# Loading the ninth token group as seven tokens a partition, one batch on each half of the partitions

## The chip, the core and the metric

The kernel runs on one core of a Trainium2 chip. The metric is the device time of one execution in microseconds (us), lower is better; three executions of the kernel before are given below. The core has five engines with instruction queues of their own: PE (TensorE, matrix products and transposes), DVE (VectorE), ACT (ScalarE), POOL (GpSimd) and SP (SyncE, which here only issues transfers), and 16 DMA engines that move data between the chip's memory and the on-chip memory of 128 partitions.

## The reference

A gated recurrence over 5056 tokens in 4 batches of 256 channels is followed by a mixture of 8 experts with 4 slots each ("soft" slots: every token takes part in every slot).

```python
sig = 1.0 / (1.0 + np.exp(-f_logit))
f = lower_bound + (1.0 - lower_bound) * sig
h = f[:, t] * h + (1.0 - f[:, t]) * x[:, t]      # for t in range(5056); y[:, t] = h

x = y.reshape(4 * 5056, 256)
logits = x @ phi                                  # 32 slots
d = softmax of logits over the tokens (axis 0)
slot_input = d.T @ x                              # 32 x 256
slot_out[e] = np.maximum(slot_input[e] @ w1[e], 0) @ w2[e]
c = softmax of logits over the slots (axis 1)
out = c @ slot_out                                # 20224 x 256, f32
```

## The kernel before

**Groups and units.** The 5056 tokens of a batch are cut into ten groups (`n_grp`) of 512 tokens; the last group begins at 5056 - 512, so the ninth (`odd`, index 8) keeps only 448 tokens. A *unit* is one group of one batch, numbered 0 to 39; units 32 to 35 are the ninth group in its four batches, and units are loaded and partly computed in pairs (32 with 33, 34 with 35). Units 8 to 31 are "long": a pair of them is two successive groups of one batch, loaded as eight tokens a partition.

**One unit, step by step.** `load` (L204) brings `f_logit` into `f_t` and `x` into `x_t` with transfers that SP issues; each tile holds a pair and each has three buffers, so SP waits until the pair three before has been used. `gate` (L227) computes the sigmoid of a pair into `s_t` on ACT. `enter` (L237) multiplies it with `x_t` into `u_t` on POOL. PE then transposes `s_t` (`s_to_channels`) and `u_t` (`u_to_channels`) from tokens on partitions to channels on partitions, two bf16 channels as one f32 value. `decay` (L286) turns the transposed sigmoid into the decay factors `a` on ACT. `scan` (L306) runs the recurrence along the tokens on DVE and writes `h`. `to_tokens` (L320) transposes `h` back on PE, `keep_tokens` (L336) copies it out of PSUM into `ht`, alternately on ACT and DVE. Once per one or two groups, `logits` multiplies `h` with `phi`, `exps` takes the exponential into `etall`, and `slots` adds up the slot inputs.

**The order of the work.** It is written out by hand, in the loop `for n in range(n_unit)` (L484): each pass issues the scan of unit n, the transposes of unit n + 1, `gate` up to four units ahead, `enter` three units ahead, and `load` six units ahead (`AHEAD`). Each engine runs its queue in that order. The weights of the experts are loaded by POOL's queue (`load_w`, L135) at the passes listed in `W_AT` (L155): one each at passes 9, 17, 25, 31 and 32, two at 33, three at 34 and six at 36; the last one comes in three pieces. They are cast from f32 to bf16 on the way.

**The ninth group.** A batch's 448 tokens are 3 x 128 + 64 (`R3` = 3, `L` = 64). Three tokens a partition of each batch of a pair go to `t[:, m, 0:3]`. The last 64 tokens of both batches share one column of 128 rows, `t[:, 0, 3]`, even rows for one batch and odd rows for the other (L216). The column is transposed once for each batch against an identity with its columns regrouped (`sides`, L252 to L256), which puts that batch's 64 tokens behind its 384.

**After the last scan.** The last groups' exponentials and slot inputs are finished, then come the experts: `hi` (first matrix, L628), transposed `ht_ps` (L643), copied into `hid` and `wide` (L646 to L660), and the second matrix for four experts at a time (L664, and L674 for the experts in `wide`). `row_sums` (L386) and filler matmuls (`spin`, L150) stand between the products. `slot_out` (L692) is the result.

**The output.** `out` is made in blocks of 16 tokens a partition (and one of 7): `whole` (L723) does one batch, `couple` (L738) two batches at a time, with copies out of PSUM on DVE and ACT. `ends` says after which token columns a part is stored; without it a couple is stored once, at its end. A couple's first part goes out as one transfer a batch (L768), a later part as one for both (L765). `rest` stores the 64 tokens that no block holds. At the start, ten small matmuls (L467 to L469) run on PE between the constants and the first unit.

Of the kernel before, what the change touches and what calls it, by code (L numbers as in the profile page):

```python
# [9 lines left out]
F32 = mybir.dt.float32  # L10
# [3 lines left out]
ACT = mybir.ActivationFunctionType  # L14
# [4 lines left out]
def kernel(  # L19
# [26 lines left out]
    def first(g):  # L46
        return g * G if g < n_grp - 1 else S - G
# [72 lines left out]
    etall = store.tile([P, S + PAD], BF16, name="etall")[:, :S]  # L120
    rrow = store.tile([P, n_grp * R, B], F32, name="rrow")
    left = store.tile([P, L, 2], BF16, name="left")
    nc.vector.memset(left, 0.0)
    csum = store.tile([P, n_grp], F32, name="csum")
    nc.vector.memset(csum, 0.0)
    w1_r = moe_w1.rearrange("e (p o) f -> e p o f", o=DC)
# [35 lines left out]
    with tc.tile_pool(name="sp2", bufs=3) as sp2, \  # L162
# [24 lines left out]
        def long(n):  # L187
            return 2 * B <= n < n_unit - 2 * B
# [15 lines left out]
        def load(n, k=2):  # L204
            for src, dst, tag in ((f_logit, fs, "f_t"), (x, xs, "x_t")):
                if n % 2 == 0:
                    dst[n // 2] = ld.tile([P, 2, R, D], F32, name=tag, tag=tag)
                t = dst[n // 2]
                if long(n):
                    g, b = place(n)  # L210
                    nc.sync.dma_start(
                        out=t.rearrange("p u r d -> p (u r) d"),
                        in_=src[b, ds(first(g), 2 * G)].rearrange("(p r) d -> p r d", r=2 * R))
                elif n // B == odd:
                    b, t0 = n % B, first(odd)
                    nc.sync.dma_start(  # L216
                        out=t[:, 0, R3],
                        in_=src[ds(b, 2), ds(t0 + P * R3, L)].rearrange("b t d -> t b d"))
                    for m in range(2):
                        nc.sync.dma_start(  # L220
                            out=t[:, m, ds(0, R3)],
                            in_=src[b + m, ds(t0, P * R3)].rearrange("(p r) d -> p r d", r=R3))
                else:
                    for m in range(n, n + k):
                        nc.sync.dma_start(out=t[:, ds(m % 2, 1)], in_=tokens(src, m, 1))
# [11 lines left out]
        def enter(n):  # L237
            uts[n] = sup.tile([P, R, D], BF16, name="u_t", tag="u_t")
            s_t, x_t = sts[n // 2][:, n % 2], xs[n // 2][:, n % 2]
            if n == 0:  # L240
                for r in range(0, R, 2):
                    nc.vector.tensor_tensor(uts[n][:, ds(r, 2)], s_t[:, ds(r, 2)],
                                            x_t[:, ds(r, 2)], ALU.mult)
            else:
                r = R3 if n // B == odd and n % 2 else R
                nc.gpsimd.tensor_tensor(uts[n][:, :r], s_t[:, :r], x_t[:, :r], ALU.mult)  # L246

        def to_channels(n, ps, t, rest):
            t = t.bitcast(F32)
            if n // B == odd:  # L250
                flat = ps.rearrange("c p r -> c (p r)")
                sides = ident_f.rearrange("p (t u) -> p u t", u=2)  # L252
                v = flat[:, ds(0, P * R3)].rearrange("c (p r) -> c p r", r=R3)
                k = P * R3 - n % 2 * L
                nc.tensor.matmul(flat[:, ds(k, P)], rest.bitcast(F32), sides,
                                 is_transpose=True, start=True, stop=True)  # L256
                for r in range(R3):
                    nc.tensor.transpose(v[:, :, r], t[:, r], ident_f)
                return
            for r in range(R):  # L260
                nc.tensor.transpose(ps[:, :, r], t[:, r], ident_f)  # L261

        def half_to_channels(n, ps, t):
            k = ds(n % 2 * (P // 2), P // 2)
            v = ps.rearrange("c p r -> c (p r)").rearrange("c (p r) -> c p r", r=2 * R)
            for r in range(2 * R):
                nc.tensor.transpose(v[:, :, r], t(r)[k].bitcast(F32), ident_f[k, k])  # L267

        def s_to_channels(n):
            if n % 2 == 0:  # L270
                pss[n // 2] = psp.tile([P, 2, P, R], F32, name="sp", tag="sp")
            to_channels(n, pss[n // 2][:, n % 2], sts[n // 2][:, n % 2],
                        sts[n // 2][:, 0, R3])

        def u_to_channels(n):
            ps = psu.tile([P, P, R], F32, name="up", tag="up")
            if long(n):
                half_to_channels(n, ps, lambda r: uts[n - n % 2 + r // R][:, r % R])
            else:
                to_channels(n, ps, uts[n], uts[n - n % 2][:, R3])  # L280
            psus[n] = ps.rearrange("c p r -> c (p r)").bitcast(BF16).rearrange(
                "c (t o) -> c t o", o=DC)

# [2 lines left out]
        def decay(n, k=2, os=range(DC)):  # L286
            T = used(n // B)
            sp = pss[n // 2].rearrange("c u p r -> c u (p r)").bitcast(BF16)
            if long(n):
                sp = sp.rearrange("c u (p r o) -> c p u r o", r=R, o=DC)  # L290
                for o in os:
                    decays[n // 2, o] = apool.tile([P, 2, G], F32, name="a", tag=f"a{o}")
                    a = decays[n // 2, o].rearrange("c u t -> c (u t)").rearrange(
                        "c (p u r) -> c p u r", u=2, r=R)
                    nc.scalar.activation(a, sp[:, :, :, :, o], ACT.Identity,  # L295
                                         scale=nomlb[:, ds(o, 1)], bias=1.0)
                return
            sp = sp.rearrange("c u (t o) -> c u t o", o=DC)
            for o in os:
                if n % 2 == 0:  # L300
                    decays[n // 2, o] = apool.tile([P, 2, G], F32, name="a", tag=f"a{o}")
                nc.scalar.activation(decays[n // 2, o][:, ds(n % 2, k), :T],  # L302
                                     sp[:, ds(n % 2, k), :T, o], ACT.Identity,
                                     scale=nomlb[:, ds(o, 1)], bias=1.0)
# [159 lines left out]
        for n in range(SINGLE):  # L464
            load(n, 1)
        lb_constants()
        for _ in range(10):  # L467
            nc.tensor.matmul(slot_bank[:, 1, ds(0, NS)], ident, ident[:, :NS],
                             start=True, stop=True, skip_group_check=True)  # L469
        gate(0, 1)  # L470
        enter(0)
        s_to_channels(0)
# [131 lines left out]
    with tc.tile_pool(name="ew", bufs=1) as ew, \  # L604
# [34 lines left out]
        for q in range(E // Q):  # L639
            ht_ps = psu.tile([P, FC, P], BF16, name="ht_ps", tag="up")  # L640
            hi_v = his[q].rearrange("p (c f) -> p f c", f=FC)
            for fc in range(FC):
                nc.tensor.transpose(ht_ps[:, fc], hi_v[:, fc], ident)  # L643
            if q == 0:
                nc.tensor.matmul(cs_ps, rep2, cs1, start=True, stop=True)
                src = ht_ps.rearrange("p f (j s) -> p f j s", s=NS)[:, :, :, ds(0, SPE)]  # L646
                src = bass.AP(tensor=src.tensor, offset=src.offset,
                              ap=[list(src.ap[0]), [P, FC], [NS + SPE, Q], [1, SPE]])
                dst = hid[:, :, :, ds(0, SPE)]
                dst = bass.AP(tensor=dst.tensor, offset=dst.offset,  # L650
                              ap=[list(dst.ap[0]), [Q * NS, FC], [NS + SPE, Q], [1, SPE]])
                nc.scalar.copy(dst, src)
                nc.vector.reciprocal(rcs, cs_ps)
                continue
            for j in range(Q):
                s0 = (Q + j) * SPE
                src = ht_ps[:, :, ds(j * NS + s0, SPE)]
                copy = nc.scalar.copy if j % 2 == 0 else nc.vector.tensor_copy
                copy(wide[:, :, j, :, ds(s0, SPE)],
                     src.unsqueeze(2).broadcast_to([P, FC, B, SPE]))  # L660
        so4_ps = pm.tile([P, D], F32, name="so4_ps", tag="pm")
        for e in range(Q):
            for fc in range(FC):
# [34 lines left out]
    with tc.tile_pool(name="osb", bufs=3) as osb:  # L698
# [39 lines left out]
        def couple(i, j, ends=()):  # L738
# [7 lines left out]
            for r in range(n_r):  # L746
# [11 lines left out]
                        scale[:, r].unsqueeze(2).broadcast_to([P, 2, D]), ALU.mult)  # L758
                if r + 1 in ends:
                    q = ds(done, r + 1 - done)  # L760
                    if done:
                        both = out[ds(2 * j * S, 2 * S)].rearrange(
                            "(u t) d -> u t d", u=2)[:, ds(t0, P * n_r)].rearrange(
                            "u (p r) d -> p u r d", r=n_r)
                        nc.sync.dma_start(out=both[:, :, q], in_=ob[:, :, q])  # L765
                    else:
                        for u in range(2):
                            nc.sync.dma_start(out=rows_of(i, 2 * j + u)[:, q],  # L768
                                              in_=ob[:, u, q])
                    done = r + 1  # L770
# [59 lines left out]
```

## Time and profile before

| | |
|---|---|
| three executions | 197.22, 197.34, 198.04 us (median 197.34) |
| the profiled execution | 197.27 us, of it span 195.5 us from first to last instruction |
| busy in the span | PE 152.8, DVE 147.2, ACT 137.3, POOL 103.3 us |
| mean granted TensorE clock | 0.859 of full speed |
| DMA | 70.75 MB written in 14145 packets; HBM read 58.23 MB, written 20.71 MB |

The page of the profile gives busy time by engine, the span in 40 slices, the DMA queues, the chain of waits that ended last, and the costliest groups of instructions. A group's line reads: source line, engine, operation, output and input tiles, shapes, count, then busy time in us and mean ns of one instruction, then the idle time of the engine before them and what ended it. A timeline's line reads: start in us, duration, engine, source line, operation and tiles, count, and in brackets the idle time before it. "w_t" and "w_sb" are the experts' weights; `SPq` is SP's queue.

### The profile page before, as it was taken

How to read it: one execution, taken by the hardware profiler on the slowest of the kernel's cores; microseconds unless marked ns; L12 is line 12 of the kernel's file. 1: busy time of each engine (PE TensorE's matmuls, PEld its weight loads, DVE VectorE, ACT ScalarE, POOL GpSimd, SP SyncE). 2: the span in 40 equal slices, each digit the busy share in tenths (PEclk: the TensorE clock that was granted, in tenths of full speed). 3: DMA queues.
4: the chain of work that ended last, by engine and by line, in shares of the span. 5: the costliest groups of instructions: out<-in, count | busy, mean ns of one | idle time of the engine just before them, and what ended most of it. 6: DMA issues, size and time to landing. Idle time of an engine off the chain costs nothing.

```text
span 195.5 us, 3260 instructions
## 1 busy us (share of the span) xinstructions
PE 152.8 (78%) x1205; PEld 105.0 (54%) x1205; DVE 147.2 (75%) x188; ACT 137.3 (70%) x188; POOL 103.3 (53%) x78
## 2 busy tenths in 40 slices
PE   1687589977998979899797887989999999990000
PEld 1465448765685767668586675557974433220000
DVE  2669858999889999999999999814279897771000
ACT  3688674899998998989987597544069987682000
POOL 2589578575999779774969969392030000000000
PEclk9999958999999999999999999999995555555555
DMA  6999999999999999999999999999939999999995
GB/s 206 421 417 424 429 424 429 429 422 393 341 424 431 416 322 427 427 408 347 366 423 413 260 213 214 215 215 213 164 148 420 427 454 419 436 432 429 429 429 221
DMA packets 14145, 70.75 MB, mean 362 GB/s; under 512 B 1569, under 2 KB 2594, under 8 KB 10162
## 3 DMA queue, kind: packets, MB, share of 16 engines
q1 hardware_dynamic: 11504, 62.13, 76.8%
q0 software_dynamic: 2624, 8.42, 21.6%
q8 instruction: 9, 0.15, 0.3%
q14 instruction: 6, 0.05, 0.1%
q10 hardware_dynamic: 2, 0.00, 0.0%
HBM read 58.23 MB, written 20.71 MB: 404 GB/s over the span
## 4 chain that ended last, share of the span: by engine, by line
PE 37%; DVE 26%; ACT 11%; DMA 8%; issue 5%; POOL 2%; SPq 0%; ACTq 0%; DVEq 0%; POOLq 0%
DVE h L313 20%; PE op L748 10%; DMA f_t<-in_f_logit_dram 8%; DVE ht L343 5%; PE hp L326 4%; ACT oc L753 4%; PE sp L261 3%; ACT s_t L235 3%; PE up L267 3%; PE lg L357 2%; POOL u_t L246 2%; PE op L711 2%; PE slot_ps L183 2%; PE so_ps L674 2%; PE slot_ps L408 1%
## 5 line engine op out<-in xcount | busy, mean ns | idle before, releaser
L246 POOL TENSOR_TENSOR u_t<-s_t,x_t 128x1024 bf16<-128x1024 bf16 (+1 forms) x39 | 82.5, 2132 | 23.6 <-ACT s_t L235 10.4
L313 DVE TENSOR_TENSOR_SCAN h<-a,h,up 128x512 bf16<-128x512 f32 (+1 forms) x72 | 87.0, 1252 | 3.5 <-PE up L267 1.8
L235 ACT ACTIVATE s_t<-f_t 128x2048 bf16<-128x2048 f32 (+2 forms) x23 | 38.3, 1668 | 4.0 <-DMA f_t<-in_f_logit_dram 3.7
L326 PE MATMUL hp<-ident_f,h 128*128 128x128 f32 (+1 forms) x160 | 29.4, 308 | 7.9 <-DVE ht L343 6.8
L326 PEld LDWEIGHTS hp<-ident_f,h 128*128 128x128 f32 (+1 forms) x160 | 23.6, 207 | 18.1 <-DVE ht L343 12.4
L748 PE MATMUL op<-slot_bd,etall 64*128 64x512 bf16 x62 | 26.4, 581 | 1.0 <-ACT oc L753 0.3
L295 ACT ACTIVATE a<-sp,lbs 128x1024 f32<-128x1024 bf16 x24 | 25.4, 1112 | 1.3 <-PE sp L261 1.0
L261 PE MATMUL sp<-ident_f,s_t 128*128 128x128 f32 x144 | 21.0, 288 | 6.7 <-ACT s_t L235 4.2
L753 ACT ACTIVATE oc<-op,rrow 128x256 f32<-128x256 f32 x54 | 22.2, 489 | 5.0 <-PE op L748 4.8
L756 DVE TENSOR_TENSOR oc<-op,rrow 128x512 f32<-128x512 f32 x35 | 22.4, 685 | 3.4 <-PE op L748 3.3
L261 PEld LDWEIGHTS sp<-ident_f,s_t 128*128 128x128 f32 x144 | 16.9, 148 | 8.8 <-ACT s_t L235 5.1
L302 ACT ACTIVATE a<-sp,lbs 128x512 f32<-128x512 bf16 (+2 forms) x22 | 17.8, 857 | 3.8 <-PE sp L261 3.5
L267 PE MATMUL up<-ident_f,u_t 64*128 64x64 f32 x192 | 17.6, 229 | 2.1 <-POOL u_t L246 2.1
L183 PE MATMUL slot_ps<-rep,ident_f 128*128 128x256 f32 x54 | 18.2, 432 | 0.6 <-POOL rep L86 0.6
L748 PEld LDWEIGHTS <-etall 64*128 64x128 bf16 x62 | 8.9, 150 | 17.4 <-issue 13.1
L343 ACT COPY ht<-hp 128x512 f32<-128x512 f32 (+1 forms) x18 | 10.5, 583 | 10.2 <-PE hp L326 10.2
L267 PEld LDWEIGHTS up<-ident_f,u_t 64*128 64x128 f32 x192 | 13.9, 138 | 6.0 <-POOL u_t L246 2.5
L343 DVE COPY ht<-hp 128x512 f32<-128x512 f32 (+1 forms) x22 | 14.7, 668 | 2.4 <-PE hp L326 2.4
L705 ACT ACTIVATE ob<-op,rrow 128x256 f32<-128x256 f32 x15 | 6.0, 475 | 7.7 <-PE op L711 7.7
L313 DVE TENSOR_TENSOR_SCAN h<-a,up 128x512 bf16<-128x512 f32 x8 | 9.3, 1208 | 2.5 <-ACT a L302 1.7
L183 PEld LDWEIGHTS slot_ps<-rep,ident_f 128*128 128x128 f32 x54 | 8.8, 199 | 3.0 <-issue 1.1
L261 PE MATMUL up<-ident_f,u_t 128*128 128x128 f32 x48 | 9.5, 329 | 0.7 <-POOL u_t L246 0.6
(110 smaller groups left out, 148.3 us busy)
## 6 DMA issues: line engine op xcount, KB each, us to landing
f_t<-in_f_logit_dram SPq DMA_DIRECT2D x12, 1024.0 KB, 11.7
x_t<-in_x_dram SPq DMA_DIRECT2D x12, 1024.0 KB, 11.1
out_dram<-oc SPq DMA_DIRECT2D x6, 2048.0 KB, 13.1
w_sb<-in_moe_w_dram POOLq DMA_DIRECT2D x14, 512.0 KB, 9.7
f_t<-in_f_logit_dram SPq DMA_DIRECT2D x12, 512.0 KB, 8.5
x_t<-in_x_dram SPq DMA_DIRECT2D x12, 512.0 KB, 8.6
out_dram<-ob SPq DMA_DIRECT2D x1, 2048.0 KB, 10.4
out_dram<-oc SPq DMA_DIRECT2D x2, 896.0 KB, 6.9
```

The costliest lines, as they stand in the source:

```text
L183: nc.tensor.matmul(slot_bank[:, 1], ident_f, wide_rep, start=False, stop=False, skip_group_check=True)
L235: nc.scalar.activation(s_t, f_t, ACT.Sigmoid, scale=-1.0)
L246: nc.gpsimd.tensor_tensor(uts[n][:, :r], s_t[:, :r], x_t[:, :r], ALU.mult)
L261: nc.tensor.transpose(ps[:, :, r], t[:, r], ident_f)
L267: nc.tensor.transpose(v[:, :, r], t(r)[k].bitcast(F32), ident_f[k, k])
L295: nc.scalar.activation(a, sp[:, :, :, :, o], ACT.Identity, scale=nomlb[:, ds(o, 1)], bias=1.0)
L313: nc.vector.tensor_tensor_scan(h[:, :T, o], decays[n // 2, o][:, n % 2, :T], up[:, :T, o], hs[number(g - 1, b)][:, ds(used(g - 1) - 1, 1), ...
L326: nc.tensor.transpose(hp[:n_p, r], hw[:, :n_p, r], ident_f)
L343: copy(hts[g][:n_p, b].rearrange("p r d -> p (r d)").bitcast(F32), hps.pop(n)[:n_p].rearrange("p r c -> p (r c)"))
L748: nc.tensor.matmul(op.rearrange("p u d -> p (u d)"), ew[:, :, r], slot_bd[ds(j * 2 * NS, 2 * NS)].rearrange("s u d -> s (u d)"), start=Tru ...
L753: nc.scalar.activation(ob[:, u, r], op[:, u], ACT.Copy, scale=scale[:, r, ds(u, 1)])
L756: nc.vector.tensor_tensor(ob[:, :, r], op, scale[:, r].unsqueeze(2).broadcast_to([P, 2, D]), ALU.mult)
```

## The change

The ninth group is loaded differently: a batch's 448 tokens go as seven tokens a partition to 64 partitions, the first batch of a pair on partitions 0 to 63 and the second on 64 to 127. What follows is adapted. The sigmoid tile is transposed as seven full columns (four written with the first unit of a pair, three with the second). The product tile is transposed in seven half columns for each unit, by the function that long units use. The decay factors are computed by two activations in place of one for each of the two channel halves, with a permuted read.

Four smaller edits come with it: one memset is done in two halves; the ten matmuls at the start are gone; the four copies into `wide` all run on DVE where every other one ran on ACT; and a part of a couple is stored by one transfer for both batches when it is the last part, rather than when it is not the first.

```diff
     left = store.tile([P, L, 2], BF16, name="left")
-    nc.vector.memset(left, 0.0)
+    for i in range(2):
+        nc.vector.memset(left[:, ds(i * L // 2, L // 2)], 0.0)
...
                 elif n // B == odd:
-                    b, t0 = n % B, first(odd)
-                    nc.sync.dma_start(
-                        out=t[:, 0, R3],
-                        in_=src[ds(b, 2), ds(t0 + P * R3, L)].rearrange("b t d -> t b d"))
                     for m in range(2):
                         nc.sync.dma_start(
-                            out=t[:, m, ds(0, R3)],
-                            in_=src[b + m, ds(t0, P * R3)].rearrange("(p r) d -> p r d", r=R3))
+                            out=t.rearrange("p u r d -> p (u r) d")[ds(m * L, L), ds(0, R + R3)],
+                            in_=src[n % B + m, ds(first(odd), used(odd))].rearrange(
+                                "(p r) d -> p r d", r=R + R3))
...
-        def to_channels(n, ps, t, rest):
+        def kept(n):
+            return R3 if n // B == odd and n % 2 else R
+
+        def to_channels(n, ps, t):
             t = t.bitcast(F32)
             if n // B == odd:
-                flat = ps.rearrange("c p r -> c (p r)")
-                sides = ident_f.rearrange("p (t u) -> p u t", u=2)
-                v = flat[:, ds(0, P * R3)].rearrange("c (p r) -> c p r", r=R3)
-                k = P * R3 - n % 2 * L
-                nc.tensor.matmul(flat[:, ds(k, P)], rest.bitcast(F32), sides,
-                                 is_transpose=True, start=True, stop=True)
-                for r in range(R3):
-                    nc.tensor.transpose(v[:, :, r], t[:, r], ident_f)
-                return
-            for r in range(R):
+                ps = ps.rearrange("c p r -> c (p r)").rearrange("c (r p) -> c p r", r=R)
+            for r in range(kept(n)):
                 nc.tensor.transpose(ps[:, :, r], t[:, r], ident_f)
 
         def half_to_channels(n, ps, t):
             k = ds(n % 2 * (P // 2), P // 2)
-            v = ps.rearrange("c p r -> c (p r)").rearrange("c (p r) -> c p r", r=2 * R)
-            for r in range(2 * R):
+            n_r = R + kept(n | 1)
+            v = ps.rearrange("c p r -> c (p r)")[:, ds(0, P // 2 * n_r)].rearrange(
+                "c (p r) -> c p r", r=n_r)
+            for r in range(n_r):
                 nc.tensor.transpose(v[:, :, r], t(r)[k].bitcast(F32), ident_f[k, k])
...
-            if long(n):
+            if long(n) or n // B == odd:
                 half_to_channels(n, ps, lambda r: uts[n - n % 2 + r // R][:, r % R])
...
+            if n // B == odd:
+                sp = sp.rearrange("c v (r u p o) -> c v u p r o", r=R, u=2, o=DC)
+                for o in os:
+                    decays[n // 2, o] = apool.tile([P, 2, G], F32, name="a", tag=f"a{o}")
+                    a = decays[n // 2, o][:, :, :T].rearrange("c u (p r) -> c u p r", r=R + R3)
+                    for v, n_r in enumerate((R, R3)):
+                        nc.scalar.activation(a[:, :, :, ds(v * R, n_r)],
+                                             sp[:, v, :, :, ds(0, n_r), o], ACT.Identity,
+                                             scale=nomlb[:, ds(o, 1)], bias=1.0)
+                return
...
         lb_constants()
-        for _ in range(10):
-            nc.tensor.matmul(slot_bank[:, 1, ds(0, NS)], ident, ident[:, :NS],
-                             start=True, stop=True, skip_group_check=True)
...
-                copy = nc.scalar.copy if j % 2 == 0 else nc.vector.tensor_copy
-                copy(wide[:, :, j, :, ds(s0, SPE)],
-                     src.unsqueeze(2).broadcast_to([P, FC, B, SPE]))
+                nc.vector.tensor_copy(wide[:, :, j, :, ds(s0, SPE)],
+                                      src.unsqueeze(2).broadcast_to([P, FC, B, SPE]))
...
                     q = ds(done, r + 1 - done)
-                    if done:
+                    if r + 1 == n_r:
                         both = out[ds(2 * j * S, 2 * S)].rearrange(
```

## The prediction

> **What bounds the kernel now.** I read the page first, its slices of DMA traffic before the chain. Columns of the second row are GB/s written in 40 slices of 4.9 us.
>
> ```profile
> DMA  6999999999999999999999999999939999999995
> GB/s 206 421 417 424 429 424 429 429 422 393 341 424 431 416 322 427 427 408 347 366 423 413 260 213 214 215 215 213 164 148 420 427 454 419 436 432 429 429 429 221
> ...
> HBM read 58.23 MB, written 20.71 MB: 404 GB/s over the span
> ```
>
> The DMA engines are full in every slice but the one around 142 us. The inputs are 2 x 20.71 = 41.4 MB, so 16.8 MB of the reads are weights, read as f32 and written as bf16 (8.4 MB in the software queue): the 213 GB/s slices are the same 426 GB/s seen from the read side. 58.23 MB at 424 GB/s is 137.3 us; the reads run from about 2 us to 142.06 us, so at most 2.8 us of that stretch is not transfer. The stores, 20.71 MB at 424 GB/s, are 48.8 us, and run from 144.1 to about 193. Next, stretches of 2 us at the seam of the two (columns: length, busy time and instructions of PE, PEld, DVE, ACT, POOL, clock, DMA share, GB/s):
>
> ```profile
> 138.00:140.00 2.00, 2.00 (x32) 1.94 (x31) 0.47 (x1) 0.00 (x0) 0.00 (x0) 1.00 1.10 198
> 140.00:142.00 2.00, 2.00 (x33) 1.71 (x31) 0.76 (x2) 0.00 (x0) 0.00 (x0) 1.00 0.51 82
> 142.00:144.00 2.00, 1.86 (x21) 1.53 (x20) 1.04 (x3) 0.46 (x2) 0.86 (x1) 1.00 0.04 12
> ```
>
> and the timeline there, where the last two products of the experts' second matrix free slot_out, without which nothing can be stored:
>
> ```profile
> 141.70 0.38 PE L674 MATMUL so_ps<-w_t,wide 128*128 128x256 bf16 x2
> ...
> 142.06 0.38 PE L674 MATMUL so_ps<-w_t,wide 128*128 128x256 bf16 x2
> ...
> 142.47 0.48 DVE L692 TENSOR_SCALAR slot_out<-so_ps,rcs 128x256 bf16<-128x256 f32 x1 [1.54 <-PE so_ps L674]
> ```
>
> The last weight piece was issued at 127.46 us and landed 14.6 us later: 142.06, the start of that product. The chain of waits shows PE there, since filler matmuls (L152) occupy it, and it shows scans before (DVE h L313 20%). But the weight stream has no slack: what lengthens the read stream by t moves the first store by t, and the stores end t later.
>
> **The loads (L214 to L225).** Units 32 to 35 hold 8 x 448 KB = 3.67 MB. The sizes and median times to landing of loads:
>
> ```profile
> f_t<-in_f_logit_dram SPq DMA_DIRECT2D x12, 1024.0 KB, 11.7
> ...
> f_t<-in_f_logit_dram SPq DMA_DIRECT2D x4, 384.0 KB, 10.2
> ...
> f_t<-in_f_logit_dram SPq DMA_DIRECT2D x2, 128.0 KB, 9.8
> ```
>
> Now each tensor of a pair takes three transfers, all to 128 partitions; afterwards two, each to 64 partitions with 7 KB in one piece. SP issues 8 instead of 12, some 0.4 us each; nothing waits for SP there but its own buffers. Bytes are equal, so the rate decides. Every kind of traffic in this trace stops at the same 424 GB/s, and every large one spans 128 partitions: 3.3 GB/s a partition, never more. No transfer to 64 partitions is there. If the cap belongs to the 16 engines, 3.67 MB take 8.65 us as now and the cost is zero. If it belongs to the partitions' side, a half takes 212 GB/s, all of it 17.3 us, and the cost is 8.65 us; the two halves of a pair stand one behind the other in SP's queue, so they do not add up to the full width by themselves. I take the upper end: the lower one needs 6.6 GB/s on a partition, twice what any row shows; the upper needs nothing unseen. Speaking against: in the weight stretches the partitions take 213 GB/s while the engines are full, so the engines' reads alone are a cap of the same size. A gain is limited too: over 88 to 99 us, with 1 KB rows among these loads, 3.99 MB were written, 4.51 MB by reads, which is 410 GB/s; removing all the shortfall from 424 saves 0.35 us.
>
> The Trainium skill, SBUF — State Buffer, section "Door 1: The DMA port swizzle (why [64,N] ≈ [32,N])", says a range of 64 partitions reaches only 8 of 16 ports, measured at 196 against 328 GB/s for 1 MiB, and that two transfers to the two halves gain 6% over one. No run here shows it yet; its two figures would make it 18.7 against 11.2 us, or +7.5 us.
>
> **Where that delay meets the work.** ACT's next steps:
>
> ```profile
> 99.44 1.70 ACT L235 ACTIVATE s_t<-f_t 128x1792 bf16<-128x1792 f32 x1
> ...
> 103.43 1.91 ACT L235 ACTIVATE s_t<-f_t 128x2048 bf16<-128x2048 f32 x1
> 106.09 0.59 ACT L343 COPY ht<-hp 128x512 f32<-128x512 f32 x1 [0.76 <-PE hp L326]
> 107.03 1.91 ACT L302 ACTIVATE a<-sp,lbs 128x896 f32<-128x896 bf16 x2 [0.35 <-PE sp L258]
> ```
>
> Issue time plus time to landing gives f of unit 34 at 97.6 us, x of 34 at 99.2, f of unit 36 at 102.5. One tensor of a pair is 2.16 us now and 4.32 then, so these come 6.5, 8.65 and 8.65 us late. The sigmoids at 99.44 and 103.43 have 1.8 and 0.9 us in hand; the second then starts 7.7 us late, and queued behind it on ACT are an ht copy and the decays of units 34 and 35, for which the scans on DVE wait. POOL's product of unit 34 (102.16) slips 5.6 us, and the weight loads of L519 queued behind it with it. They cannot leave the engines idle: x of the last pair (113.0 us now) lands about 121.6, and by then four more weights, 1.05 MB read or 2.5 us each, stand behind it. So the work slips about 7.7 us and the weight stream 8.65; the stream still ends last, and the step is 8.65, not the sum.
>
> **The other edits.** By forms:
>
> ```profile
> L302 ACT ACTIVATE a<-sp,lbs 128x512 f32<-128x512 bf16 x12 | 7.6, 678 | 2.0 <-PE sp L261 2.0
> L302 ACT ACTIVATE a<-sp,lbs 128x896 f32<-128x896 bf16 x4 | 3.8, 1008 | 0.4 <-PE sp L258 0.4
> ```
>
> - Decays: each of the 4 activations of 896 elements becomes 512 + 384. From 678 (512) and 1117 ns (1024) the slope is 0.857 ns, so 384 costs 568 ns: 1246 instead of 1008, +0.95 us on ACT in all, in stalls that the late loads make anyway; if those were absent, ACT still idles 2.0 us at 109 to 111. The permuted read (p, r swapped) has a row: L295 permutes too, 1112 against 1117 ns in order.
> - Transposes: s loses 2 of 16 (0.11 us each in the chain); each of 4 units' u goes from 4 wide (0.44 us) to 7 half ones (8 take 0.65, so 0.57): net +0.3 us on PE, again within those stalls. Even units now need the odd one's u_t, as long units do already: u of 35 was ready at 106.5, the scan of 34 starts at 110.1.
> - Four wide copies on DVE: 4 x 224 ns from 135.06 end at 135.96; so4's copy starts at 136.06 and PE needs the first at 135.9. Zero; without that cover, 0.4 us.
> - The ten matmuls at 2.77 to 3.22 us: PE then waits for ACT until 5.50, and the chain is input transfers until 17.1. Zero. If they set when PE speeds up (four transposes 1.11 us before about 13 us, 0.66 after), one or two groups would be 0.45 us slower each; bound 0.9 us, covered by waits for f_t (3.5 us).
> - Memset in halves: 0.11 us on a DVE idle until 5.7.
> - Stores: eight L768 transfers become four of the same bytes. Work ends at 176.9 us, the engines at about 193, so saved issues (0.33 to 1.2 us on SP) lie under a backlog of 16 us. The two-batch form exists already (768 KB in 5.7 us, against 896 KB in 6.9). Zero, +-0.3 at the uneven end of the last transfer.
>
> Sum against the profiled execution (197.27: span 195.5 and 1.8 around it; the median is 197.34, the same): 197.27 + 8.65 = 205.9.
>
> **Rivals.**
> - Out of phase. Engines that are ahead write to one half while the others write to the other; with half of the width regained the cost is 4.3 us, 201.6. For: in-flight loads overlap by 7 to 10 us to landing. [...]
> - No price: the cap is the engines'. Then 197.3, within 0.7. For: the weight stretches above. Against: the per-partition bound.
> - Faster: SP is what holds the read stream up. The four transfers of L216 take it 0.55 to 0.66 us each to issue, 2.3 us in all; without them the last twelve loads are queued up to 2.3 us sooner, and if half of that fills gaps of the stream (it has 2.8 us at most that is not transfer), the end comes at 196.1. It decides only if the engines ran short between 79 and 104 us and half-width transfers run at the full rate. Against: the DMA share is full in those slices.
> - Slower still: PE starves while loads are late and its clock falls. It was granted 0.50 at 26 to 30 us, after two stretches of 2 us with PE busy 0.80 and 0.79; DVE lost 0.5 + 1.3 us of those 4. With 2 us on the path: 207.9. Against: slack of 0.95 us between work and weights.
>
> **Numbers.** Half rate 0.62 (205.9, 203.5 to 207); out of phase 0.16 (199 to 203.5); slower still 0.08; no price 0.09, of it 0.07 within 0.5% and 0.02 faster; faster as above 0.05. A measurement here tells 0.5%, about 1 us, from no change. Slower is 0.62 + 0.16 + 0.08 = 0.86, same 0.07, faster 0.02 + 0.05 = 0.07. The first two cases hold 0.78; with the nearer part of the third, up to 208.3, it is 0.8. Low 199.0.
>
> **What would show it.** Loads of 448 KB landing late, GB/s near 212 for 17 us from about 88 us with the DMA share full; waits of ACT and POOL for f_t and x_t there; the last weight near 150.7; first store near 152.7; stores of 4096 KB at the same 424 GB/s; four wide copies done before so4's. Wrong, if those stretches stay at 400 or more, if the last weight comes by 143, or if PE's clock falls between 95 and 140 us.

## The result, and the profile after

The changed kernel takes 206.36 us (median of six executions, 204.9 to 206.83) against 197.69 for the kernel before in the same series (197.22 to 198.9). The ratio is 1.0423, 95% interval 1.0389 to 1.0456: slower by 8.3 us on the 197.3 of the kernel before (7.7 to 9.0); the two medians differ by 8.7. The forecast was 205.9, in a range of 199.0 to 208.3. The profiled execution took 206.52 us, 204.8 of it span.

The slices of the page, as for the kernel before:

```profile
DMA  5999999999999999999999999999938999999996
GB/s 208 421 419 420 429 431 426 421 429 319 420 434 421 333 411 423 424 191 239 239 218 358 355 258 222 212 213 215 207 59 358 422 448 413 448 416 429 442 413 259
...
HBM read 58.23 MB, written 20.71 MB: 386 GB/s over the span
```

A slice is 5.1 us here. The bytes are the same and the DMA share is as full, but four slices (17 to 20, counted from 0: 87 to 107 us) move 191 to 239 GB/s where the kernel before moved 347 to 423. In longer stretches (the last three columns are clock, DMA share and GB/s):

```profile
88.00:96.00 8.00, 6.84 (x80) 5.15 (x79) 8.00 (x9) 5.28 (x6) 4.85 (x3) 1.00 1.00 215
96.00:104.00 8.00, 5.79 (x55) 4.01 (x51) 5.62 (x5) 4.62 (x5) 2.90 (x2) 1.00 1.04 242
104.00:109.00 5.00, 1.85 (x12) 1.62 (x13) 2.30 (x4) 4.07 (x6) 0.85 (x1) 0.92 1.00 210
```

The stretch from 88 to 109 us writes 8 x 215 + 8 x 242 + 5 x 210 = 4.71 MB in 21 us; that is 224 GB/s, where the kernel before wrote 3.99 MB in the 11 us from 88 to 99, 363 GB/s. The issues of the loads:

```profile
f_t<-in_f_logit_dram SPq DMA_DIRECT2D x4, 448.0 KB, 17.5
x_t<-in_x_dram SPq DMA_DIRECT2D x4, 448.0 KB, 17.3
```

They take 17.5 us to land where the 384 KB ones took 10.2. What ACT waits for now (start, duration, line, operation, and in brackets the idle time before):

```profile
95.95 1.70 ACT L233 ACTIVATE s_t<-f_t 128x1792 bf16<-128x1792 f32 x1 [2.69 <-DMA f_t<-in_f_logit_dram]
...
104.93 1.70 ACT L233 ACTIVATE s_t<-f_t 128x1792 bf16<-128x1792 f32 x1 [4.31 <-POOL u_t L244]
...
111.76 1.91 ACT L233 ACTIVATE s_t<-f_t 128x2048 bf16<-128x2048 f32 x1 [2.33 <-DMA f_t<-in_f_logit_dram]
```

The sigmoids of units 34 and 36 stood at 99.44 and 103.43. The 4.31 us are put down to POOL; the two f loads of unit 34, though, were issued at 84.4 and 84.9 and took 18.5 and 19.9 us, so the second landed at 104.8: the load is what came last there too. And the end of the weight stream:

```profile
151.39 0.38 PE L674 MATMUL so_ps<-w_t,wide 128*128 128x256 bf16 x2
...
151.81 0.48 DVE L692 TENSOR_SCALAR slot_out<-so_ps,rcs 128x256 bf16<-128x256 f32 x1 [2.18 <-PE so_ps L674]
```

142.06 became 151.39 and slot_out moved from 142.47 to 151.81, 9.34 us. The first store followed, before and after (five issues in a line):

```profile
144.09 3.10 SPq L735 DMA_DIRECT2D out_dram<-ob  x5
...
153.45 3.00 SPq L735 DMA_DIRECT2D out_dram<-ob  x5
```

The span grew by 9.3. The chain that ended last, by engine, shows the transfers now, before and after:

```profile
PE 37%; DVE 26%; ACT 11%; DMA 8%; issue 5%; POOL 2%; SPq 0%; ACTq 0%; DVEq 0%; POOLq 0%
...
DMA 55%; PE 13%; POOL 12%; ACT 5%; issue 4%; DVE 0%; ACTq 0%; SPq 0%; POOLq 0%
```

After the first store the two kernels are alike: from 156 to 190 us the stores run at 433 GB/s before and 429 after.

### The profile page after: what moved, and what is told of

The parts are those of the page before. It is cut to its first block, busy times and chain, and to the rows that moved or that the text cites. A ratio compares the mean times of both kernels' runs of the same rounds, so it can differ in the third digit from the quotient of the medians.

```text
span 204.8 us, 3253 instructions
## 1 busy us (share of the span) xinstructions
PE 155.7 (76%) x1205; PEld 107.1 (52%) x1205; DVE 147.4 (72%) x191; ACT 137.2 (67%) x190; POOL 103.2 (50%) x78
## 4 chain that ended last, share of the span: by engine, by line
DMA 55%; PE 13%; POOL 12%; ACT 5%; issue 4%; DVE 0%; ACTq 0%; SPq 0%; POOLq 0%
DMA x_t<-in_x_dram 41%; POOL u_t L244 10%; PE op L748 9%; DMA w_sb<-in_moe_w_dram 8%; DMA w_t<-in_moe_w_dram 7%; ACT oc L753 3%; PE op L711 2%; POOL w_sb L138 2%; ACT ob L705 1%; PE sp L254 0%; PE up L262 0%; PE slot_ps L184 0%; PE hp L330 0%; PE op L779 0%; POOL w_sb L148 0%
## 5 line engine op out<-in xcount | busy, mean ns | idle before, releaser
L254 PE MATMUL sp<-ident_f,s_t 128*128 128x128 f32 x158 | 24.9, 304 | 6.5 <-ACT s_t L233 4.6
L254 PEld LDWEIGHTS sp<-ident_f,s_t 128*128 128x128 f32 x158 | 20.2, 157 | 8.7 <-ACT s_t L233 5.2
L262 PE MATMUL up<-ident_f,u_t 64*128 64x64 f32 x220 | 20.5, 230 | 2.2 <-POOL u_t L244 2.1
L262 PEld LDWEIGHTS up<-ident_f,u_t 64*128 64x128 f32 x220 | 16.1, 138 | 6.8 <-POOL u_t L244 2.8
L748 PEld LDWEIGHTS <-etall 64*128 64x128 bf16 x62 | 9.0, 151 | 17.5 <-issue 13.2
L306 ACT ACTIVATE a<-sp,lbs 128x512 f32<-128x512 bf16 (+1 forms) x18 | 14.0, 825 | 4.6 <-PE sp L254 4.6
## 6 DMA issues: line engine op xcount, KB each, us to landing
out_dram<-ob SPq DMA_DIRECT2D x1, 2048.0 KB, 10.2
f_t<-in_f_logit_dram SPq DMA_DIRECT2D x4, 448.0 KB, 17.5
```

The costliest lines, as they stand in the source:

```text
L748: nc.tensor.matmul(op.rearrange("p u d -> p (u d)"), ew[:, :, r], slot_bd[ds(j * 2 * NS, 2 * NS)].rearrange("s u d -> s (u d)"), start=Tru ...
```

## The experiments

**The loads without the smaller edits, and the smaller edits alone.** The first undoes four pieces of the diff, the second applies only them (shortened at `...`):

```diff
-    nc.vector.memset(left, 0.0)
+    for i in range(2):
+        nc.vector.memset(left[:, ds(i * L // 2, L // 2)], 0.0)
...
-        for _ in range(10):
-            nc.tensor.matmul(slot_bank[:, 1, ds(0, NS)], ident, ident[:, :NS],
...
-                copy = nc.scalar.copy if j % 2 == 0 else nc.vector.tensor_copy
...
+                nc.vector.tensor_copy(wide[:, :, j, :, ds(s0, SPE)],
...
-                    if done:
+                    if r + 1 == n_r:
```

> The changed kernel with its four smaller edits undone (memset, ten matmuls at the start, wide copies, stores of couples as before). Width theory (the rate belongs to the partitions that a transfer reaches, so two half transfers cost twice one whole): 206 to 207, the whole slowdown of about 8.7 us, with 185 to 260 GB/s between 87 and 109 us. Rival, the smaller edits: then about 197.5, or a part of the 8.7 between.

> The kernel before with the four smaller edits alone. Width theory: 197.5, within 0.3%, last weight used at 142 us. Rival, the merged stores or the missing matmuls cost or save something that the late loads hid: a difference of over 0.5 us either way.

Measured: loads alone 205.98 us, ratio 1.0404 (1.0353 to 1.0456); edits alone 197.77 us, ratio 1.0009 (0.9986 to 1.0032), slot_out at 142.75 against 142.47. The whole slowdown is in the ninth group's path, and the stores as merged transfers (4096 KB) cost and save nothing that shows.

**The same layout through all 128 partitions.**

```diff
-                    for m in range(2):
-                        nc.sync.dma_start(
-                            out=t.rearrange("p u r d -> p (u r) d")[ds(m * L, L), ds(0, R + R3)],
-                            in_=src[n % B + m, ds(first(odd), used(odd))].rearrange(
-                                "(p r) d -> p r d", r=R + R3))
+                    nc.sync.dma_start(
+                        out=t.rearrange("p u r d -> p (u r d)")[:, ds(0, (R + R3) * D)],
+                        in_=src[ds(n % B, 2), ds(first(odd), used(odd))].rearrange(
+                            "b (p r) d -> p b (r d)", r=R + R3))
```

> The changed kernel with one load for each tensor of a pair over all 128 partitions, 7 KB in one piece to each, the two batches on alternating partitions; the later steps are left as they are, so the tokens of the two batches are mixed in the ninth group and only the time counts. Width theory: 197.0 to 198.2, the slowdown is gone though the decays (three quarters of a microsecond longer on ACT for each pair), the half transposes and the waits for both products stay. Rival, layout (the new transposes, decays and waits cost it): 203 or more. Rival, long pieces (7 KB pieces are slow): no gain, 205 or more.

Measured: 197.2 us, ratio 0.9989 (0.9966 to 1.0011). The slowdown is gone. In the packet records of the trace a 7168-byte piece of these loads takes 272 ns here, and 504 ns in the changed kernel (medians of 512 pieces; in the changed kernel a tenth took under 393 and a tenth over 630). Its slices from the page's list:

```profile
GB/s 209 418 420 420 430 426 423 430 426 347 386 426 426 404 338 425 423 427 343 392 417 394 264 219 213 213 214 213 159 162 420 426 448 426 430 430 430 430 430 218
```

No slice at half rate is left among the loads; 343 to 394 are slices with weights among them, counted at half, and the slices near 214 are the weights alone, as before the change. So neither the new transposes, the longer decays nor the wait for both products costs time that shows, and 7 KB pieces are as fast as 8 KB ones (26 bytes a ns: 7168 / 272, as 8192 / 309).

**Other loads in halves, and in columns.** Units 28 to 31, which the change does not touch:

```diff
+                    for ps, rs in parts if n >= n_unit - 3 * B else ((slice(0, P), slice(0, 2 * R)),):
+                        nc.sync.dma_start(out=o_v[ps, rs], in_=i_v[ps, rs])
...
# halves:  parts = ((slice(0, 64), slice(0, 8)), (slice(64, 128), slice(0, 8)))
# columns: parts = ((slice(0, 128), slice(0, 4)), (slice(0, 128), slice(4, 8)))
```

> The kernel before, where the loads of units 28 to 31 (four of 1 MB, 128 partitions, 8 KB in one piece) are each two transfers of 64 partitions; nothing else changes. Width theory: 4.19 MB at 212 instead of 424 GB/s, +9.9 us, 207.4 (206 to 209), less what the loads of the ninth group behind them win back. Rival, layout and later steps: no change, 197.5. Out of phase (half of the width comes back): about +5, 202.5.

> The kernel before, where the same four loads of units 28 to 31 are split as often, into two transfers of 512 KB, but by token columns: both go to all 128 partitions, 4 KB in one piece. Width theory: no change, 197.4 (within 0.5%). Rival, it is the number or the size of the transfers that cost 10.7 us when the loads were split by halves: 207 or more.

Measured: halves 208.09 us, ratio 1.0520 (1.0458 to 1.0582), +10.3 us on 197.35; columns 197.75 us, ratio 1.0015 (0.9998 to 1.0032). The slices, first by halves and then by columns:

```profile
GB/s 211 420 420 420 432 423 426 426 426 319 426 426 424 322 422 203 224 226 215 286 411 421 412 234 213 214 214 213 210 69 359 421 442 416 442 410 455 410 455 210
```

```profile
GB/s 210 419 421 420 434 420 429 427 423 368 368 423 430 406 331 416 419 414 340 371 422 414 258 215 214 214 214 213 160 163 415 431 444 425 429 429 429 429 429 218
```

By halves the slow slices (203 to 226) start at 77 us, two slices earlier than in the changed kernel, where those loads are; by columns none is slow. As many transfers of the same size cost nothing when each goes to all partitions. 4.19 MB cost 10.3 us here, 2.4 us a MB; 3.67 MB cost 8.3 in the change, 2.3 a MB.

**A split by other partitions.** The same loads as 32 to 95, 0 to 31 and 96 to 127 (`parts = ((slice(32, 96), ...), (slice(0, 32), ...), (slice(96, 128), ...))`, shortened at `...`).

> The kernel before, where the same four loads are split by partitions into three: 32 to 95 (512 KB), 0 to 31 and 96 to 127 (256 KB each). If the width is that of the two halves 0 to 63 and 64 to 127, whose paths the first transfer reaches both: it runs at 424 GB/s (1.24 us), the others at 212 (1.24 us each), 3.7 us a load instead of 2.47, +4.9 in all: 202.3 (201 to 203.5). Rival, the rate simply goes with the number of partitions (3.3 GB/s each): three times 2.47 us, 7.4 a load, +19.8: 217. Rival, as slow as by halves: 208. The Trainium skill, SBUF — State Buffer, section on Door 1, has partitions 32 to 95 on all 16 ports, 0 to 31 and 96 to 127 on 8 each, as in the first case.

Measured: ratio 1.0534 (1.0475 to 1.0593), 10.5 us more, as slow as by halves. The first case, 202.3, is what the rule of the two halves gives, and it is wrong for this queue.

**Quarters in turn.**

```diff
-                    for m in range(2):
+                    for lo in (0, 64, 32, 96):
+                        m, p0 = lo // L, lo % L    # 32 partitions and 224 tokens each
...
```

> The changed kernel, where each half transfer of the ninth group is two of 32 partitions, issued in the order 0 to 31, 64 to 95, 32 to 63, 96 to 127, so that pieces for the two halves alternate in one queue. Width theory with transfers strictly one behind the other: as the changed kernel, 206 (205 to 207.5). Rival, short pieces for different halves overlap in flight: half of the width comes back, 201 to 203.

Measured: 203.71 us, ratio 1.0312 (1.0276 to 1.0348): 6.2 us of the 8.3 are left, a quarter is won back. It lies between the two expectations, nearer to the second. Alternating shorter transfers helps a little; that pieces for the two halves overlap in flight is a reading of this and not shown.

**Rates alone.** Because of that miss, two runs, of one execution each, measured shapes by themselves, ahead of the first unit, into places that weights overwrite later (from the first run; `shapes` stands for its list of first partition, number of partitions and width).

```diff
+        for i, (p0, n_p, w) in enumerate(shapes):
+            for j in range(4)[::1 - i % 2 * 2]:
+                v = x[j, ds(0, 4 * n_p)].rearrange("(p r) d -> p (r d)", r=4)
+                nc.sync.dma_start(out=spare[j][ds(p0, n_p), ds(0, w)], in_=v[:, ds(0, w)])
```

> The kernel before with seven groups of four loads of their own put ahead of the first unit, each group waiting for the one before, all into places that the weights overwrite later: 4 KB in one piece to each of partitions 0 to 127, 0 to 63, 64 to 127, 32 to 95, 0 to 95, 0 to 31 and 0 to 111 (each group's pieces 16 bytes shorter than those of the last, so that they can be told apart). Only the rates inside the groups count. All of 128: 424 GB/s, 159 ns a piece. If the rate goes with the number of partitions reached: 212 for each half and for 32 to 95, 318 for 0 to 95, 106 for 0 to 31, 371 for 0 to 111. If it goes with the two halves 0 to 63 and 64 to 127 (the Trainium skill, SBUF — State Buffer, Door 1): 212 for the halves and for 0 to 31, 424 for 32 to 95. The runs so far speak for the first on 32 to 95 and leave 0 to 31 open.

Stretches inside the groups (all 128; the two halves one after the other; 0 to 95; 0 to 31; 0 to 111):

```profile
3.00:7.00 4.00, 0.25 (x10) 0.14 (x6) 0.13 (x2) 0.00 (x0) 0.70 (x2) 1.00 1.01 379
12.00:19.00 7.00, 0.00 (x0) 0.00 (x0) 0.00 (x0) 0.00 (x0) 0.00 (x0) 1.00 1.03 213
...
29.50:33.50 4.00, 0.00 (x0) 0.00 (x0) 0.00 (x0) 0.00 (x0) 0.00 (x0) 1.00 1.02 261
36.00:37.50 1.50, 0.00 (x0) 0.00 (x0) 0.00 (x0) 0.00 (x0) 0.00 (x0) 1.00 0.82 238
42.00:47.00 5.00, 0.00 (x0) 0.00 (x0) 0.00 (x0) 0.00 (x0) 0.00 (x0) 1.00 1.00 281
```

213 GB/s for the halves, half of the 426 of full stretches. But 0 to 31 runs at 238, not at 106: the rate does not go with the number of partitions. And 0 to 95 (261) and 0 to 111 (281, with some loads of the kernel's own among them; 284 over 44 to 46 us, nearly all its own) are slower than the 318 and 371 that the number would give. The two halves do not explain these either: both ranges reach both halves, and even if the fuller half set the pace at 212 GB/s, its 64 of 96 or 112 partitions would make 318 and 371 again. The 64 partitions 32 to 95 are too short a group for a stretch; 199 of their 256 pieces took 130 to 170 ns, as pieces to all 128 do (159), where pieces to 0 to 63 took 313 (median) and to 64 to 127 320.

> As the probe before, six groups of 2.1 MB of loads, 4 KB in one piece to each partition, each group behind the one before it: (a) eight to 32 to 95; (b) four times 32 to 95, 0 to 31, 96 to 127; (c) four times 96 to 127, 32 to 63, 64 to 95, 0 to 31; (d) four times 0 to 63, 64 to 127; (e) eight to 0 to 63; (f) four to all 128. Only the rates inside the groups count. If the width is that of the halves 0 to 63 and 64 to 127 and transfers go one behind the other: (a) 424 GB/s, pieces of 159 ns; (b) half of the bytes at 424 and half at 212, 283; (c), (d), (e) 212; (f) 424. If pieces of one transfer meet those of the next: (b) and (c) between 212 and 424, the shorter the transfers the nearer to 424. If every transfer that is not to all 128 partitions runs at half rate: all but (f) 212. The run split by 32 to 95 (+11 us) speaks for the last in (b), the probe before (199 of 256 pieces to 32 to 95 took 170 ns or less) for the first in (a).

Groups (a) to (f) in order:

```profile
3.00:9.00 6.00, 0.21 (x8) 0.10 (x4) 0.10 (x2) 0.00 (x0) 0.70 (x2) 1.00 0.88 315
13.00:20.00 7.00, 0.00 (x0) 0.00 (x0) 0.00 (x0) 0.00 (x0) 0.00 (x0) 1.00 0.88 240
23.00:30.00 7.00, 0.00 (x0) 0.00 (x0) 0.00 (x0) 0.00 (x0) 0.00 (x0) 1.00 0.87 245
34.00:40.00 6.00, 0.00 (x0) 0.00 (x0) 0.00 (x0) 0.00 (x0) 0.00 (x0) 1.00 1.05 230
45.00:52.00 7.00, 0.00 (x0) 0.00 (x0) 0.00 (x0) 0.00 (x0) 0.00 (x0) 1.00 1.02 204
56.00:61.00 5.00, 0.00 (x0) 0.00 (x0) 0.00 (x0) 0.00 (x0) 0.00 (x0) 1.00 1.03 416
```

32 to 95 alone (a) moves 315 GB/s over 6 us that are not filled (share 0.88; single microseconds reach 389), its pieces taking 159 ns in the median; 0 to 63 alone (e) moves 204, pieces 316 ns; all 128 (f) 416, pieces 156 ns. So a transfer to one half runs at half rate, and one that lies across both halves need not. Mixed with transfers to 0 to 31 and 96 to 127 (b), that gain is all but lost: 240, not 283. Short transfers that alternate (c) get 245, alternating halves (d) 230. No one rule fits all of this. The two halves fit the pieces of (a), (e), (f) and 0 to 31, but not 0 to 95, 0 to 111 or (b); "about half rate for whatever is not to all 128 partitions" fits all but 32 to 95 alone. For the changed kernel, whose transfers each go to one half, both say the same. Which of them holds was not settled: the packet records do not say which DMA engine moved a piece.

**The weight stream as the bound.**

```diff
# one weight less, in the changed kernel
+            if i == 2 * E - 1:
+                w2_sb[E - 1] = w2_sb[E - 2]
+                return
...
# one weight twice, in the kernel before
+                if n == 33:
+                    load_w(1)
```

> The changed kernel without the load of the last expert's second matrix, 1.05 MB of reads (the expert before it is used in its place, so the last expert's output is another). If the weight stream sets the end and the work ends before it: 2.5 us less, 203.5 (203.2 to 204.2). Rival, the late work sets the end as much as the stream: less than 1 us gained, 205.4 or more.

> The kernel before, where pass 33 loads one weight a second time, the same bytes to the same place: 1.05 MB more of reads at full width, and nothing else. If the read stream sets the end, as the prediction has it: 2.47 us at 424 GB/s, 199.9 (199.3 to 200.3). Rival, the work sets the end and the stream has room: under 0.7 us, 198.1 or less.

Measured: one weight less gives 205.8 us, ratio to the kernel before 1.0435 (1.0382 to 1.0489), not to be told from the changed kernel; its span is 1.2 us shorter (203.6), slot_out at 150.60. The 2.5 us expected are a miss. One weight more gives 199.75 us, ratio 1.0099 (1.0063 to 1.0135): 1.2 to 2.7 us, which clears the rival's 0.7. Its slot_out in the profile is 2.43 us later than the 142.47 of the kernel before, for 2.47 expected:

```profile
144.90 0.48 DVE L694 TENSOR_SCALAR slot_out<-so_ps,rcs 128x256 bf16<-128x256 f32 x1 [2.20 <-PE so_ps L676]
```

PE in the run with one weight less:

```profile
143.35 1.03 PE L677 MATMUL so_ps<-w_sb,wide 128*128 128x256 bf16 x8 [1.53 <-DMA w_sb<-in_moe_w_dram]
...
145.79 1.03 PE L677 MATMUL so_ps<-w_sb,wide 128*128 128x256 bf16 x8 [0.47 <-DMA w_sb<-in_moe_w_dram]
...
148.25 1.03 PE L677 MATMUL so_ps<-w_t,wide 128*128 128x256 bf16 x8
```

PE still waits for the weights before the last one, 2.44 us apart, and behind the third come its own products and fillers up to 150.6 without a wait. In the profiles, lengthening the stream moved slot_out in full; shortening it at its tail gained 1.2 us, and then PE's own queue was the bound.

## Why the prediction was right

**The bound.** The longer stream of reads moved the first store by as much as the last weight (144.09 to 153.45, 9.4 us, against 9.3), and a stream lengthened by other bytes moved slot_out in the same way (+2.43 of 2.47). That part is shown.

**The term of 8.65 us.** It was the upper end of a range that began at zero, and the upper end is what the runs show: 8.3 us by the ratio, 9.3 in the profiled execution. In the halves alone it is 204 GB/s against 416, a factor of 2.04. The reason given for choosing that end, that no row shows more than 3.3 GB/s on a partition, was not the right one: 0 to 31 runs at 238 GB/s, 7.4 on a partition. That the wrong reason led to the right end is luck: the change happens to send each transfer to exactly one half. The Trainium skill's page SBUF — State Buffer, section Door 1, which the prediction set beside its sum, says that the rate goes with how many of 16 ports a range of partitions reaches: 8 for 0 to 31 and for 0 to 63 alike. The runs agree there, with 238 GB/s for 0 to 31 and 204 to 213 for the halves. By its table 32 to 95 reaches all 16, and its pieces by themselves are at full speed; but 0 to 95 and 0 to 111 reach all 16 as well and moved 261 and 281, which that rule does not give. The Trainium skill's "+6%" for two transfers to the two halves stands on the same page under "Can I just issue two DMAs to hit both halves?"; here the gain is 13% when they alternate (230 against 204) and 4% when four follow four (213).

**Out of phase.** The rival at 201.6 did not come. Alternating transfers regain a little (230 GB/s against 204), and with four short transfers in turn 2.1 us of 8.3.

**Where the delay meets the work.** The load of unit 34's f was forecast 6.5 us late and came 7.2 late (97.6 to 104.8); the sigmoid of unit 36 moved by 8.3 (103.43 to 111.76), forecast 7.7. POOL's product of unit 34 was forecast 5.6 late and came 7.6 late (102.16 to 109.71). The work behind did win back some: the start of the experts (sin on DVE) moved from 131.03 to 137.35, 6.3 us, against 9.3 of the weight stream, so PE waits for w_sb, 1.65 us at its first product. The clock did fall, which the prediction named as something that would make it wrong: 0.57 in the mean from 108 to 112 us, after PE had been idle from 104 to 107. That sign was too strict: the work that it slowed still reached the experts 3 us less late than the weights, so the fall lay under the weight stream and shows in no measured time.

**The slack of 0.95 us** between work and stream was put on the kernel before. The run with one weight less has 1.2 us of it in the changed kernel (slot_out at 150.60 instead of 151.81), which that run's own expectation of 2.5 us left out.

**Mis-sized terms, hidden as said.** A pair of decay activations was put at 1246 ns and takes 767 + 659 = 1426:

```profile
L298 ACT ACTIVATE a<-sp,lbs 128x512 f32<-128x512 bf16 x4 | 3.1, 767 | 0.0
L298 ACT ACTIVATE a<-sp,lbs 128x384 f32<-128x384 bf16 x4 | 2.6, 659 | 0.0
```

Each is about 90 ns longer than in order (678, and 568 by the slope), at both sizes. The row that the prediction leaned on (L295) reads in another order, and it writes without gaps; the new activations also write in runs of four or three of seven, and no run separates the two. The run with full-width loads, which keeps them, shows no cost. The four copies into `wide` took 0.62 us, not 0.9, and waited 0.88 us for POOL's memset of `wide`, which stands behind the late weight loads in POOL's queue: a wait that the prediction did not have, covered by PE's wait for w_sb. The ten matmuls: the first four transposes of PE that take 0.66 us or less, where those before take about 1.1, begin between 14.4 and 16.9 us in five runs that have them and in the kernel before, and between 14.2 and 17.1 us in five runs without, so they do not set that point. The stores were as forecast.

## What to carry to other kernels

Where transfers are the bound, load every tile through all 128 partitions: putting two batches on the two halves doubled the time of those loads here, although the bytes were the same, the transfers fewer and the pieces longer. When one tile has to hold two sources, alternate them over the partitions in one transfer, if the later steps can take that order; the run that did so shows the time of it, and no run here has later steps made for it.

An edit whose unknown is a rate can be priced before it is run: take the lowest and the highest rate that the profile leaves open, and divide the bytes by each. The difference counts in full where the queue that it lengthens has no gaps.

## What the runs showed of the hardware that was not expected

- A transfer to 32 partitions moves as fast as one to 64 (238 GB/s over 1.5 us for 0 to 31, against 204 to 213 for the halves), and one to 112 partitions reaches only 281, far from 7/8 of 426.
- 32 to 95 by itself has full-speed pieces (159 ns for 4 KB), but in a queue with 0 to 31 and 96 to 127 the whole stays at 240 GB/s, and the kernel split so is as slow as by halves.
- An activation that reads its input with the two orders swapped, and writes in runs of four or three, is some 90 ns longer than one in order, with 512 elements as with 384.
